# Attention beside a gated MLP on one core: the last of four pattern tiles made in place by a DMA that adds a constant

## The chip, the cores and the metric

The kernel runs on one core of a Trainium2 chip. The metric is the device time in microseconds of one execution; lower is better. A time is the median of several executions. One further execution is recorded by the hardware profiler; its lines are quoted as the profile prints them, with PE for TensorE, PEld for its weight loads, DVE for VectorE, ACT for ScalarE, POOL for GpSimd and SP for SyncE.

## The reference

One block of attention and one gated block read the same 2048 rows of 512, and a sigmoid gate mixes them:

```
q, k, v = split((x @ wqkv), 32 heads of 16)
scores  = einsum("bhqd,bhkd->bhqk", q, k) * 16 ** -0.5
a = merge_heads(softmax(scores) @ v) @ wo
b = ((x @ w_gate) * (x @ w_up)) @ w_down        # inner width 1376
g = sigmoid((x * gate_w).sum(-1, keepdims=True))
out = g * a + (1 - g) * b
```

All inputs and the output are bfloat16.

## The kernel before, in words

**Tiling.** The 2048 queries are four chunks of 512, the 32 heads are four blocks of eight, and of a block either the even or the odd four heads are taken together: that is a "quad", 32 in all. For a quad the 2048 keys are 16 key tiles of 128. One quad with one key tile is a "step", 512 in all, and a step has four score tiles of 128 keys x 512 queries, one for each head. The PE array is used as two halves of 64 rows, each split in four groups of 32 columns: `pe64` (L1616) issues a set of four matmuls on one half (recorded at L1620).

**Two ways to an exponential.** An A step goes to ScalarE: `exp` (L1709, recorded at L1718) reads one or two score banks and writes bfloat16 tiles. A D step goes to VectorE: `dpass` (L1747, recorded at L1754) adds a constant to the scaled score and writes it as int16, whose bits are read as a bfloat16; this is a piecewise linear exponential. To make it better, four such tiles with different "patterns" are used. The first is the tile y itself, 128 x 2048 int16 for the four heads. The three others are y + 32, y + 64 and y + 96, which are a quarter, a half and three quarters of an octave further. Each is multiplied with its own scaled copy of V (`Vs`), and the four products are summed on PE. `copy` (L1756) makes the others, on DVE (recorded at L1760) as a whole or on POOL (L1764) as a whole or in halves, each into a tile buffer of its own. There are eight such buffers in `DB`, and the buffers `wv` and `wk` join them once their weights are no longer needed. D steps are allowed for six of the 16 key tiles of a quad (`dks`); those that are not taken so are done on ACT.

**PV.** `pv` multiplies a finished pattern tile with V and adds it into PSUM bank 7 until a quad's 16 key tiles are done. An A step needs one PV set for each half, a D step four.

**What sets the order.** `_Sched` is a planner in Python that runs when the kernel is built. It goes through time with assumed durations, hands each engine its next piece of work, and so writes a fixed list of instructions for each engine. `_Plan.emit` (L48) turns the dependences between the lists into semaphore waits. On the chip each engine works through its list in order and waits where an operand isn't there yet. The planner's choices are steered by tables in `PAR` (L2055): each is a list of (number of windows, value), a window being 4 us of planned time. The tables named later: `acc` (L2057), how many first D steps of a quad get the treatment below; `alook` and `alook2` (L675, L700), how many score tiles for ACT may be outstanding when scores are put ahead of PV and fill work, and behind it; `dl` and `dend` (`next_d`, L218), how many D steps a quad may take and when it stops.

On POOL, `try_pool` (L972) takes a step's missing copies from the last pattern backwards; on DVE, `copy_dve` (L908) takes them from the first forwards. POOL's queue also holds the multiplications that normalise the output (recorded at L1923). SP's queue holds almost all transfers: the masked queries (`QM<-qraw`), the denominators, the rows of `oc`, weights and results.

**A path that is switched off.** With `acc` over 0, a step that is marked (L244, L245) makes only patterns two and three by `copy`. Once PV of the first pattern is done on both halves and both copies are made (`y_unref`, L506), `acc_pool` (L960) has POOL issue a DMA that adds 96 to the tile y in place:

```
src = bass.AP(c.tensor, c.offset, [[0, 128], [1, 2048]])
return self.P.dma("pool", lambda e: e.dma_start(self.db[buf], src, accum_op=ALU.add),
                  deps + [self.r["cst"]], "dacc%d" % buf)
```

The source is one row of 2048 int16 in device memory, read for every partition. In the planner POOL is taken for `aiss` 0.9 us, the tile is booked as ready `alat` 3.9 us after that, and two such tiles at least 2.65 us apart:

```
self.pool_v = self.lock_v = self.now + self.par["aiss"]
t = self.dma_v = max(self.pool_v + self.par["alat"], self.dma_v + 2.65)
for r in (0, 1):
    self.vq[r].append((t, e, 3, [op]))
```

The other work (projections, the gated block, the output projection) fills PE between scores and PV, in sets of the same shape, and DVE empties its banks.

Of the kernel before, what the change touches and what calls it, by code (L numbers as in the profile page):

```python
# [1548 lines left out]
class _Hw:  # L1549
# [376 lines left out]
    def prologue(self):  # L1926
# [119 lines left out]
        if self.par["acc"]:  # L2046
# [7 lines left out]

PAR = {'NA': 14,  # L2055
 'ND': 8,
 'acc': 0,  # L2057
 'adel': 0.1,
 'aiss': 0.9,
 'alat': 3.9,  # L2060
 'alook': ((13, 2), (5, 6), (8, 4), (6, 2), (9, 4), (3, 5), (21, 2), (3, 3), (3, 2), (1, 4), (5, 2), (18, 5),
           (6, 2), (6, 4), (5, 5), (13, 2), (4, 5), (6, 2), (2, 4), (3, 3), (7, 4), (26, 6), (7, 2)),
 'alook2': ((18, 4), (5, 3), (9, 0), (6, 2), (3, 0), (3, 3), (3, 0), (5, 5), (1, 3), (2, 0), (5, 6), (11, 3),
            (3, 5), (9, 3), (6, 2), (6, 6), (6, 5), (1, 4), (29, 0), (4, 6), (5, 2), (7, 0), (10, 4), (10, 0),
            (13, 4)),
 'amax': ((7, 5), (35, 4), (6, 5), (81, 4), (6, 5), (45, 4)),
 'amin': ((7, 3), (6, 2), (13, 4), (6, 2), (9, 3), (3, 2), (6, 4), (2, 2), (22, 3), (28, 4), (5, 3), (18, 4),
          (7, 3), (5, 4), (5, 2), (19, 4), (5, 3), (5, 4), (9, 3)),
 'apick': ((38, 0), (6, 1), (3, 0), (6, 1), (2, 0), (2, 1), (4, 0), (12, 1), (1, 0), (12, 1), (5, 0), (1, 1),
           (5, 0), (14, 1), (11, 0), (25, 1), (14, 0), (6, 1), (13, 0)),  # L2070
 'ares': ((5, 1), (6, 2), (3, 1), (21, 2), (3, 1), (6, 2), (7, 1), (1, 2), (8, 1), (17, 2), (15, 1), (6, 0),
          (24, 2), (9, 1), (9, 0), (22, 2), (18, 1)),
 'await': ((2, 0.05), (10, 0), (6, 0.05), (5, 0), (6, 0.2), (3, 0), (3, 0.2), (3, 0.1), (3, 0.2), (3, 0),
           (7, 0.05), (1, 0.2), (8, 0.05), (11, 0), (3, 0.2), (6, 0), (3, 0.4), (6, 0.05), (3, 0.1), (10, 0),
           (5, 0.4), (4, 0.2), (10, 0.05), (1, 0.4), (3, 0), (15, 0.05), (2, 0.2), (19, 0.05), (3, 0.4),
           (8, 0), (8, 0.2)),
 'cpmax': ((2, 10), (9, 6), (24, 8), (3, 5), (6, 8), (11, 2), (5, 3), (11, 6), (1, 5), (10, 10), (17, 14),
           (3, 2), (19, 8), (1, 14), (5, 6), (6, 14), (2, 10), (5, 5), (22, 8), (12, 3), (6, 8)),
 'dact': ((13, 2), (13, 3), (18, 2), (16, 3), (12, 2), (30, 3), (19, 2), (4, 3), (22, 2), (14, 3), (1, 2),
          (12, 3), (6, 2)),  # L2080
 'dahead': ((7, 0), (34, 1), (14, 0), (35, 1), (3, 0), (4, 1), (5, 0), (59, 1), (10, 0), (9, 1)),
 'dend': ((2, 2), (3, 3), (2, 1), (10, 0), (6, 3), (1, 4), (2, 1), (11, 4), (7, 3), (6, 2), (21, 3), (6, 4),
          (3, 0), (7, 4), (2, 2), (3, 4), (10, 0), (9, 4), (10, 2), (1, 3), (15, 1), (5, 3), (5, 2), (14, 0),
          (1, 4), (12, 3), (6, 2)),
 'dks': [2, 4, 7, 9, 12, 14],
 'dl': ((2, 3), (3, 4), (2, 6), (5, 4), (5, 6), (3, 5), (62, 6), (5, 4), (7, 6), (5, 5), (3, 6), (5, 4),
        (10, 6), (5, 5), (5, 6), (4, 5), (5, 6), (1, 5), (10, 6), (5, 4), (9, 6), (10, 5), (9, 6)),
 'dlook': ((29, 1), (3, 2), (70, 1), (9, 2), (1, 1), (15, 2), (13, 1), (2, 2), (19, 1), (5, 2), (14, 1)),
 'dlook2': ((2, 0), (11, 3), (5, 0), (14, 1), (6, 2), (6, 1), (8, 2), (5, 4), (4, 0), (2, 4), (8, 3), (3, 0),
            (8, 1), (5, 4), (3, 0), (2, 3), (10, 2), (9, 1), (10, 0), (4, 1), (4, 0), (11, 4), (2, 1), (5, 3),  # L2090
            (5, 0), (5, 4), (5, 0), (18, 3)),
 'dmaq': 2.0,
 'dmax': ((5, 2), (18, 3), (3, 2), (15, 3), (14, 2), (16, 3), (3, 2), (3, 3), (3, 2), (3, 3), (7, 2), (8, 3),
          (4, 2), (9, 3), (29, 2), (2, 3), (5, 2), (19, 3), (1, 2), (3, 1), (10, 2)),
 'dpair': ((17, 1), (6, 2), (3, 0), (15, 1), (14, 0), (13, 1), (6, 2), (9, 0), (4, 2), (7, 0), (1, 2), (2, 1),
           (5, 2), (9, 0), (10, 1), (10, 0), (6, 1), (10, 0), (18, 1), (1, 0), (14, 1)),
 'dpri': ((13, 1), (31, 0), (20, 1), (1, 0), (6, 1), (26, 0), (5, 1), (40, 0), (5, 1), (25, 0), (8, 1)),
 'dresv': ((67, 0), (7, 1), (7, 2), (99, 0)),
 'dwait': ((2, 0.4), (11, 0), (5, 0.2), (5, 0.4), (3, 0.1), (12, 0.2), (6, 0), (7, 0.2), (1, 0), (8, 0.2),
           (11, 0.4), (3, 0.2), (9, 0.4), (6, 0.2), (8, 0.1), (14, 0), (10, 0.2), (21, 0.4), (5, 0),  # L2100
           (14, 0.2), (6, 0.1), (3, 0), (1, 0.1), (9, 0)),
 'fcf': ((7, 1), (34, 0), (3, 1), (136, 0)),
 'fdebt': ((2, 0), (12, -10), (12, 25), (6, -30), (9, 0), (1, -30), (6, 0), (12, -10), (5, 25), (6, -30),
           (3, 0), (9, 25), (3, 10), (9, 0), (7, 25), (9, 0), (10, 10), (8, 25), (6, 0), (2, 10), (5, -10),
           (5, 10), (14, 25), (5, 0), (1, 10), (3, -10), (10, 10)),
 'ffn0': 2.6,
 'ffn1': 31.5,
 'flead': ((2, 160), (3, 0), (15, 80), (3, 160), (15, 80), (6, 160), (7, 20), (1, 160), (8, 20), (2, 80),
           (9, 10), (6, 80), (15, 160), (10, 10), (5, 40), (4, 160), (18, 80), (5, 20), (3, 0), (3, 20),
           (7, 160), (14, 80), (13, 40), (6, 80)),  # L2110
 'fmax': ((18, 3), (8, 2), (18, 3), (6, 2), (21, 1), (12, 2), (9, 3), (10, 1), (19, 3), (1, 2), (5, 3),
          (10, 2), (43, 3)),
 'fres': ((44, 0), (16, 2), (29, 0), (13, 2), (28, 0), (2, 2), (10, 1), (38, 0)),
 'fs2': ((13, 1), (22, 0), (3, 1), (6, 0), (20, 1), (10, 0), (6, 1), (3, 0), (6, 1), (3, 0), (9, 1), (20, 0),
         (4, 1), (10, 0), (5, 1), (22, 0), (18, 1)),
 'fstart': ((20, 2), (6, 1), (1, 2), (15, 1), (18, 2), (2, 1), (9, 2), (3, 1), (13, 2), (7, 1), (39, 2),
            (4, 1), (43, 2)),
 'fuse': 0,
 'fv': ((7, 1), (10, 0), (10, 1), (5, 0), (12, 1), (16, 0), (11, 1), (18, 0), (23, 1), (27, 0), (8, 1),
        (14, 0), (19, 1)),  # L2120
 'g0': 3,
 'gdue': 1.5,
 'gfull': ((2, 0.9), (24, 0.6), (6, 0.3), (9, 1.9), (3, 0.9), (3, 1.6), (4, 0.3), (16, 1.6), (10, 2.5),
           (15, 1.2), (10, 1.6), (15, 0.3), (14, 1.9), (4, 0.9), (5, 0.6), (7, 0.3), (14, 0.6), (1, 0.3),
           (5, 1.2), (13, 0.6)),
 'ghalf': ((7, 0.7), (1, 0.5), (17, 1.2), (1, 0.7), (15, 0.5), (3, 0.9), (3, 0.3), (5, 1.2), (1, 0.9),
           (14, 0.3), (5, 0.7), (6, 0.5), (5, 0.7), (19, 0.3), (19, 0.5), (8, 0.7), (5, 0.5), (6, 9),
           (7, 0.5), (10, 1.2), (8, 0.3), (2, 0.5), (13, 1.2)),
 'gwin': ((18, 0), (8, 1.2), (18, 0.5), (7, 1.2), (2, 0.5), (6, 1.2), (3, 0.2), (21, 1.2), (7, 0), (11, 1.2),
          (10, 0.5), (14, 1.2), (4, 0.5), (2, 1.2), (9, 0.8), (2, 0.5), (5, 1.2), (5, 0), (14, 0.5), (1, 1.2),  # L2130
          (13, 0)),
 'hold': 1,
 'klead': 0.9,
 'kp': [1, 4, 7],
# [3 lines left out]
 'npre': 0,  # L2138
 'olead': 0.9,
 'ov': [[], [], [], []],  # L2140
 'pfirst': ((22, 0), (4, 1), (12, 0), (33, 1), (3, 0), (28, 1), (5, 0), (12, 1), (2, 0), (9, 1), (32, 0),
            (10, 1), (8, 0)),
 'ph': 1,
 'pool0': 13.0,
 'pre0': 25.0,
# [7 lines left out]
 'retire2': 150.0,  # L2153
 'retire3': 50.0,
 'rmarg': 0.3,
 'skew': ((18, 3), (5, 2), (12, 4), (3, 2), (3, 4), (6, 2), (15, 3), (5, 2), (14, 6), (1, 2), (5, 4), (3, 3),
          (2, 1), (10, 3), (19, 1), (8, 2), (3, 6), (4, 4), (4, 6), (7, 1), (14, 3), (6, 1), (13, 2)),
 'skewd': ((2, 4), (11, 2), (14, 3), (8, 4), (3, 1), (3, 4), (3, 2), (8, 3), (29, 2), (8, 3), (12, 2), (1, 3),
           (19, 4), (4, 3), (3, 2), (12, 1), (7, 4), (5, 3), (11, 2), (4, 4), (3, 3), (10, 4)),
 'sp0': 19.5,  # L2160
 't0': 8.2,
 'tw': [(('wk', False), 0), (('wq', False), 0), (('wk', True), 20), (('wq', True), 22), (('wv',), 12),
        (('gw',), 13.5)],
 'tx': [6.5, 12, 16.5, 20.5],
 'ugdur': 1.131,
 'vpref': ((13, 2), (64, 0), (15, 3), (9, 0), (1, 2), (24, 0), (3, 1), (8, 0), (3, 1), (27, 0), (13, 3)),
 'warmto': 0.0,
 'wgap': 1.2,
 'xd': ((7, 20), (6, 6), (7, 4), (3, 2), (3, 6), (18, 2), (16, 20), (2, 2), (9, 4), (3, 6), (18, 4), (9, 6),
        (1, 20), (19, 2), (4, 4), (4, 2), (6, 4), (5, 8), (7, 2), (14, 6), (5, 2), (14, 6)),  # L2170
 'xk': ((5, 4), (7, 2), (1, 4), (4, 0), (7, 1), (2, 4), (16, 1), (2, 4), (3, 2), (5, 0), (10, 4), (11, 0),
        (1, 2), (9, 1), (14, 0), (5, 4), (5, 3), (10, 1), (14, 4), (6, 1), (3, 0), (7, 3), (14, 0), (5, 3),
        (1, 4), (5, 1), (8, 4)),
 'xq': 0,
 'xw': 0}


def bass_gated_mix__mha_block__glu_gated_bilinear__prompt_kernel(
    nc: bass.Bass,
    A_x: bass.AP,  # L2180
    A_wqkv: bass.AP,
    A_wo: bass.AP,
# [41 lines left out]
```

## Time and profile before

| | us |
|---|---|
| median of 3 executions | 710.07 |
| their range | 707.67 to 713.38 |
| the profiled execution | 708.04 |
| its span, first to last instruction | 706.3 |
| ACT busy in it | 684.8 |
| DVE busy | 645.9 |
| POOL busy | 450.7 |

The granted clock of TensorE is 1.00 throughout. Busy times count an engine's instructions as the profiler records them; PE's matmuls overlap, so that its busy time is not a measure of how full it is. In a group's line the count follows the x, then come busy time, mean nanoseconds of one, idle time of the engine just before such an instruction, and what ended that idle time. In a wait line come total, number and longest.

### The profile page before, as it was taken

How to read it: one execution, taken by the hardware profiler on the slowest of the kernel's cores; microseconds unless marked ns; L12 is line 12 of the kernel's file. 1: busy time of each engine (PE TensorE's matmuls, PEld its weight loads, DVE VectorE, ACT ScalarE, POOL GpSimd, SP SyncE). 2: the span in 40 equal slices, each digit the busy share in tenths (PEclk: the TensorE clock that was granted, in tenths of full speed). 3: DMA queues.
4: the chain of work that ended last, by engine and by line, in shares of the span. 5: the costliest groups of instructions: out<-in, count | busy, mean ns of one | idle time of the engine just before them, and what ended most of it. 6: DMA issues, size and time to landing. Idle time of an engine off the chain costs nothing.

```text
span 706.3 us, 47734 instructions
## 1 busy us (share of the span) xinstructions
PE 692.3 (98%) x22103; PEld 358.7 (51%) x22103; DVE 645.9 (91%) x1060; ACT 684.8 (97%) x820; POOL 450.7 (64%) x351
## 2 busy tenths in 40 slices
PE   8999999999999999999999999999999999999997
PEld 4564555554444545554554445555553555555553
DVE  5999999899999999999998998999999978989985
ACT  6899999999999999999999999999999999999994
POOL 3365658877464666655675747777666788487630
PEclk9999999999999999999999999999999999999999
DMA  9202341003010100001000010100001010000101
GB/s 156 69 6 57 78 107 36 6 20 94 16 35 5 35 18 23 28 11 28 13 23 23 15 33 19 36 13 13 27 7 40 12 36 24 14 23 18 29 19 33
DMA packets 33752, 22.97 MB, mean 33 GB/s; under 512 B 19500, under 2 KB 30156, under 8 KB 33552
## 3 DMA queue, kind: packets, MB, share of 16 engines
q1 hardware_dynamic: 32416, 18.86, 11.1%
q8 instruction: 173, 2.83, 1.6%
q0 software_dynamic: 176, 0.53, 0.3%
q10 hardware_dynamic: 960, 0.52, 0.3%
q14 instruction: 27, 0.22, 0.1%
HBM read 11.71 MB, written 2.36 MB: 20 GB/s over the span
## 4 chain that ended last, share of the span: by engine, by line
PE 90%; DVE 3%; ACT 3%; issue 1%; DMA 1%; ACTq 0%; DVEq 0%
PE ps L1620 90%; DVE DB L1754 2%; ACT xT L1718 1%; ACT PT L1718 1%; DVE DB L1760 1%; DMA DB<-in_A_x_dram 1%; ACT wu L1718 0%; DVE wv L1754 0%; DVE oc L1830 0%; DVE hT L1902 0%; PE ps L2017 0%; ACTq L1933 0%; DVE wu L1813 0%; ACT wd L1718 0%; ACT QM L2030 0%
## 5 line engine op out<-in xcount | busy, mean ns | idle before, releaser
L1620 PE MATMUL ps<-QM,KT 64*32 64x512 bf16 x8192 | 496.6, 379 | 4.2 <-issue 1.3
L1764 POOL TENSOR_TENSOR DB<-DB,cadd 128x512 int32<-128x512 int32 (+1 forms) x207 | 280.2, 1373 | 146.9 <-DVE DB L1760 62.0
L1718 ACT ACTIVATE PT<-ps 128x1024 bf16<-128x1024 f32 (+1 forms) x394 | 358.5, 1016 | 1.6 <-PE ps L1620 0.7
L1754 DVE TENSOR_SCALAR DB<-ps 128x512 int16<-128x512 f32 (+1 forms) x493 | 327.7, 692 | 31.8 <-PE ps L1620 28.3
L1620 PE MATMUL ps<-DB,Vs 64*17 64x512 bf16 x2856 | 261.6, 377 | 0.7
L1718 ACT ACTIVATE xT<-ps 128x1024 bf16<-128x1024 f32 (+1 forms) x270 | 258.6, 1043 | 1.9 <-PE ps L1620 1.7
L1620 PEld LDWEIGHTS ps<-QM,KT 64*32 64x32 bf16 x8192 | 152.2, 89 | 177.9 <-ACT PT L1718 46.9
L1620 PE MATMUL ps<-PT,Vp 64*17 64x512 bf16 x1444 | 204.5, 376 | 0.3 <-issue 0.2
L1620 PE MATMUL ps<-xT,Vp 64*17 64x512 bf16 x1030 | 165.3, 376 | 0.2
L1620 PE MATMUL ps<-xT,wu 64*32 64x512 bf16 x1376 | 111.9, 377 | 0.0
L1620 PE MATMUL ps<-xT,wg 64*32 64x512 bf16 x1376 | 110.5, 377 | 1.0 <-issue 0.9
L1760 DVE TENSOR_SCALAR DB<-DB 128x2048 int16<-128x2048 int16 (+1 forms) x160 | 107.3, 701 | 0.6 <-PE ps L1620 0.2
L1620 PE MATMUL ps<-wd,hT 64*32 64x512 bf16 x1408 | 100.2, 377 | 0.1
L1620 PE MATMUL ps<-DB,Vp 64*17 64x512 bf16 x1000 | 97.0, 377 | 0.6 <-DVE oc L1830 0.2
L1620 PEld LDWEIGHTS ps<-DB,Vs 64*17 64x17 bf16 x2856 | 70.6, 87 | 37.0 <-PE ps L1620 10.5
L1718 ACT ACTIVATE wd<-ps 128x1024 bf16<-128x1024 f32 (+1 forms) x69 | 65.7, 1059 | 0.6 <-PE ps L1620 0.4
L1764 POOL TENSOR_TENSOR DB<-wv,cadd 128x512 int32<-128x512 int32 (+1 forms) x38 | 49.7, 1331 | 24.2 <-DVE wv L1754 9.6
L1620 PEld LDWEIGHTS ps<-PT,Vp 64*17 64x17 bf16 x1444 | 51.2, 87 | 17.9 <-PE ps L1620 4.6
L1764 POOL TENSOR_TENSOR wv<-DB,cadd 128x512 int32<-128x512 int32 (+1 forms) x31 | 42.1, 1371 | 19.7 <-DVE DB L1760 7.8
L1754 DVE TENSOR_SCALAR wv<-ps 128x512 int16<-128x512 f32 x72 | 47.6, 683 | 2.5 <-PE ps L1620 2.1
L1764 POOL TENSOR_TENSOR wk<-DB,cadd 128x512 int32<-128x512 int32 (+1 forms) x30 | 39.4, 1324 | 15.8 <-DVE DB L1760 11.2
L1620 PEld LDWEIGHTS ps<-xT,Vp 64*17 64x17 bf16 x1030 | 40.8, 87 | 11.6 <-PE ps L1620 2.6
(108 smaller groups left out, 839.5 us busy)
## 6 DMA issues: line engine op xcount, KB each, us to landing
rb<-rscr SPq DMA_DIRECT2D x16, 256.0 KB
QM<-qraw SPq DMA_DIRECT2D x124, 16.0 KB, 2.3
oc<-oraw SPq DMA_DIRECT2D x60, 32.0 KB, 2.2
out_dram<-ost SPq DMA_DIRECT2D x12, 128.0 KB, 1.7
wd<-in_B_w_down_dram SPq DMA_DIRECT2D x10, 128.0 KB, 2.5
wu<-in_B_w_up_dram SPq DMA_DIRECT2D x12, 96.0 KB, 2.2
wg<-in_B_w_gate_dram SPq DMA_DIRECT2D x12, 96.0 KB, 2.6
wv<-in_A_wqkv_dram POOLq DMA_DIRECT2D x1, 512.0 KB, 5.2
```

Of the source, the lines that this page charges most:

```text
L1620: o = pe.matmul(dst, lhs, rhs, start=st, stop=sp, tile_position=(64 * r, 32 * cc), skip_group_check=True)
L1718: return self.P.op("act", lambda a: a.activation(dst, src, ACT.Exp, scale=self.ES), deps)
L1754: return self.dve(lambda v: v.tensor_scalar(dst, src, self.YB, 0.0, ALU.add, ALU.max), deps)
L1760: return self.dve(lambda e: e.tensor_scalar(o, a, 32.0 * v, None, ALU.add), deps)
L1764: lambda e: e.tensor_tensor(o.bitcast(I32), a.bitcast(I32), self.cadd[:, v, :].bitcast(I32).to_broadcast([128, n]), ALU.add),
```

## The change

The code of the kernel stays as it is; only the dictionary `PAR` changes. `acc` becomes a table instead of 0, so that the path described above is taken for the first two to four D steps of a quad (the entry that holds at the planned time), with 1 in two windows. In a marked step one of the three copies is not made, the DMA on POOL takes its place, and the step needs three tile buffers instead of four. In the prologue one POOL memset and two small stores on SP write the row of 96s. All other tables of the planner are replaced as well, so that the order of work on every engine is a different one, while scalars such as `aiss` and `alat`, the list `dks` and the number of buffers stay. Means over the 180 windows, before and after: `acc` 0 and 3.28, `alook` 3.59 and 2.26, `alook2` 2.49 and 3.90, `dl` 5.56 and 5.61, `dend` 2.21 and 1.97.

```diff
 PAR = {'NA': 14,
  'ND': 8,
- 'acc': 0,
+ 'acc': ((2, 2), (3, 3), (2, 2), (10, 3), (20, 4), (29, 3), (1, 4), (3, 3), (14, 4), (2, 3), (4, 4), (27, 3),
+         (25, 4), (6, 2), (19, 3), (4, 4), (5, 2), (1, 1), (1, 4), (2, 2)),
  'adel': 0.1,
  'aiss': 0.9,
  'alat': 3.9,
- 'alook': ((13, 2), (5, 6), (8, 4), (6, 2), (9, 4), (3, 5), (21, 2), (3, 3), (3, 2), (1, 4), (5, 2), (18, 5),
-           (6, 2), (6, 4), (5, 5), (13, 2), (4, 5), (6, 2), (2, 4), (3, 3), (7, 4), (26, 6), (7, 2)),
...
+ 'alook': ((122, 2), (3, 4), (42, 2), (10, 6), (3, 2)),
...
- 'dl': ((2, 3), (3, 4), (2, 6), (5, 4), (5, 6), (3, 5), (62, 6), (5, 4), (7, 6), (5, 5), (3, 6), (5, 4),
-        (10, 6), (5, 5), (5, 6), (4, 5), (5, 6), (1, 5), (10, 6), (5, 4), (9, 6), (10, 5), (9, 6)),
...
+ 'dl': ((2, 3), (3, 5), (16, 6), (1, 4), (2, 6), (3, 5), (11, 6), (3, 5), (3, 4), (2, 5), (16, 6), (4, 5),
+        (4, 6), (4, 5), (3, 6), (8, 5), (2, 4), (1, 5), (14, 6), (5, 5), (9, 6), (1, 5), (46, 6), (1, 4),
+        (2, 5), (1, 3), (4, 5), (2, 3), (2, 5), (5, 6)),
...
```

## The prediction, made before the changed kernel was run

> **What bounds the kernel now.** I read the page's busy table first, then the groups with each shape apart for ACT and POOL, then the busy times by stage, then the wait lists of PE's loads and of POOL, and last the DMA issues.
>
> ```profile
> PE 692.3 (98%) x22103; PEld 358.7 (51%) x22103; DVE 645.9 (91%) x1060; ACT 684.8 (97%) x820; POOL 450.7 (64%) x351
> 300.00:325.00 25.00, 25.00 (x872) 13.70 (x864) 24.36 (x41) 25.00 (x28) 14.02 (x15) 1.00 0.07 16
> 425.00:450.00 25.00, 25.00 (x860) 13.55 (x855) 22.34 (x34) 25.00 (x29) 19.07 (x11) 1.00 0.10 25
> ```
>
> The columns of the stage lines after the length are PE, PEld, DVE, ACT and POOL busy, granted clock, DMA share and GB/s. ACT has no idle time in most stages between 50 and 675 us; its idle is at the two ends. PE's 98% is not PE at its peak: the same page counts 22103 matmuls in sets of four, two half-arrays run side by side, and sets on one half start 0.216 us apart in the timeline (301.29, 301.50, 301.72), so 22103/4/2 x 0.216 = 597 us would hold them. PE's queue stands in between, and for whom is in its wait list:
>
> ```profile
> PEld ps L1620 <- ACT PT L1718: 47.4, 187, 0.8
> PEld ps L1620 <- ACT xT L1718: 35.3, 131, 0.8
> PEld ps L1620 <- DVE DB L1754: 31.7, 130, 0.6
> PEld ps L1620 <- PE ps L1620: 29.0, 91, 0.6
> ...
> PEld ps L1620 <- ACT wd L1718: 7.1, 30, 0.4
> PEld ps L1620 <- DVE wv L1754: 4.9, 20, 0.5
> ```
>
> It waits for score banks that ACT's exp (L1718) or DVE's passes (L1754) have not emptied. The four-pattern copies stand almost nowhere: PE waits for DVE's copies (L1760) 0.9 us in all, and in the answer on POOL's copies (L1764) the list of who waited for them is empty. POOL itself waits for others about 255 us.
>
> ```profile
> L1760 DVE TENSOR_SCALAR DB<-DB 128x2048 int16<-128x2048 int16 x150 | 103.0, 717 | 0.6 <-PE ps L1620 0.2
> ...
> L1764 POOL TENSOR_TENSOR DB<-DB,cadd 128x1024 int32<-128x1024 int32 x81 | 152.3, 1893 | 79.2 <-DVE DB L1760 32.7 <-PE ps L1620 27.3 <-DVE DB L1754 13.7
> L1764 POOL TENSOR_TENSOR DB<-DB,cadd 128x512 int32<-128x512 int32 x126 | 128.0, 1039 | 67.7 <-DVE DB L1760 29.4 <-PE ps L1620 18.6 <-DVE wv L1760 14.1
> ```
>
> So the time is ACT's score tiles plus two ends. By shape ACT has 649 exps of two tiles and 158 of one: 1456 tiles, 364 of the 512 steps (quad, key tile). DVE's passes by shape are 486 + 72 + 20 of one tile (into DB, wv and wk) and 7 of two: 592 tiles, so 148 D steps, 4.6 per quad. A step on ACT costs (684.8 - 8)/364 = 1.86 us of it. Whatever the change does, the end moves only if ACT gets fewer steps, or if PE's queue stands longer.
>
> **The change part by part.** The sum is made against the profiled execution, 708.04 us (span 706.3 and 1.74 around it); the median of the runs shown, 710.07, lies 2.0 above it. The forecast is the median plus the sum (a profiled execution would stand 2 lower).
>
> How many tiles. The acc table's mean over its 180 windows of 4 us is 3.28; times 32 quads is 105; a quad that has fewer D steps than its entry loses some, so I take 100 of the 444 copies (148 x 3; by the groups DVE made 219 whole and 15 half, POOL 118 whole and 199 half, which gives 226.5 + 217.5 = 444).
>
> Removed: POOL takes a step's copies from the last backwards, so the ones removed are mostly POOL's: 424.5 us over 217.5 tiles is 1.95 each, 195 us; if they were all DVE's it would be 157/226.5 = 0.69 each, 69 us. Directly this is worth nothing: nobody waits for POOL's copies.
>
> Added on POOL: 100 DMA issues. The nearest rows are POOL's two own DMA issues, 0.757 us (wv) and 0.913 us (gw), so 76 to 91 us. POOL is left with some 110 us more.
>
> Moved: with these 110 us POOL can make 110/1.95 = 56 copies that DVE makes now, 39 us of DVE. That could become D steps in place of A steps: one costs DVE 4 x 0.685 and half of its copies, 1.5 x 0.69, together 3.8, so ten steps, each 1.86 us off ACT: 19 us at best. PE pays six more sets each, 10 x 6 x 0.216/2 = 6.5 us, of 109 us that its queue now stands. At worst it is nothing: the tables that ration D steps hardly differ (dl 5.56 before, 5.61 after, in the mean). Between 0 and -19 I take -6, three steps, as the row it is nearest to is the rationing, which barely moves.
>
> The landing. The last pattern's PV can't be ordered against a copy of 0.6 to 1.9 us any more. It needs, in turn: PV of the first pattern on both halves and both other copies (they read the tile), POOL's turn (behind up to 1.89 us of a copy), the issue, and the landing. The order is written for 0.9 us of issue and 3.9 us after it, 4.8 in all, and 2.65 us between two of them. No row shows a DMA that adds. The nearest is POOL's plain 512 KB load, 5.2 us to landing in a stage where the DMA engines were 85% busy; POOL's 1 KB load took 4.2.
>
> ```profile
> wv<-in_A_wqkv_dram POOLq DMA_DIRECT2D x1, 512.0 KB, 5.2
> ...
> gw<-in_gate_w_dram POOLq DMA_DIRECT2D x1, 1.0 KB, 4.2
> ```
>
> From below, 4.2 is early by 0.6 and costs nothing. From above, the tile must be read as well as written; page part 3 gives 2.83 MB for 1.6% and 0.53 MB for 0.3% of 16 engines' span, 0.57% per MB, so 0.5 MB is 2.1 us of all engines and a second movement makes 7.3, late by 2.5. I take 5.2, late by 0.4, as it has the same queue and size. PE issues in order, so a late PV stops both halves, and behind it wait scores that feed ACT and DVE. If each of 100 were due at once: 40 us. Ready PVs of other steps are booked ahead of many; I let two in five show: +16.
>
> POOL's queue: behind an accumulate that waits for PV stand the next steps' copies and 16 normalisations (L1923, 1.28 us). Their cover is that nobody waits for POOL's copies now; if it goes, the price is that of a late PV and is within the 16. SP's queue is not passed; its transfers (QM 2.3 us, oc 2.2) share engines with 100 x 2.1 = 210 us of new transfers, 30% of the span on a present 13.4% by part 3; they run a quad ahead, 22 us, so 0. The y tile stays held till the landing, but a step takes three tiles, not four: 0. Prologue: one more memset and two 2 KB stores on SP, none before the first scores: 0.
>
> The order. All tables of the written order are new. First-rank lookahead of ACT's scores falls from a mean of 3.59 to 2.26, so PVs and fills go ahead of scores once two are out; second-rank rises from 2.49 to 3.90. Two tiles are one exp of 1.07 us. From ACT's idle after PE (under 10 us) to 0.03 us at each of some 800 exps, this is 0 to +24, and better pairing (158 single exps at 0.62, 0.53 each in pairs) could give -14. I take +2. Sum: -6 + 16 + 2 = +12, **722 us**.
>
> Two pages of the Trainium skill bear on it. DMA: Bandwidth & Descriptors (section "Anatomy of one DMA — SWDGE (gpsimd) path") fits such a DMA as 2.0 us plus bytes over 436 GB/s: 3.2 us for 512 KB, with an issue of 0.8 about 4.0, an estimate under the 4.8 booked. By it the landing would cost nothing and the sum would be -4; the row here, 5.2, disagrees, though among other traffic. SBUF — State Buffer (section "Who interferes with whom") says that descriptor generation on GpSimd is starved while DVE runs a two-port copy. POOL's 88.7 us of idle until DVE's copies agrees with a plan that keeps the two apart; if they still meet, each issue would lengthen by one DVE copy, and the landing with it.
>
> **The rivals.** First, faster: the landing is in time (4.8 or under from issue), and the freed DVE time does become D steps. For it: PE waits 38.9 us for passes, which fewer copies on DVE bring forward, and the DMA engines are nearly idle now (mean 33 GB/s). Against: the rationing tables. -8 to -19, so 14 off: 696 us. It decides if ACT's steps fall below about 360. Second, no difference: the relief is POOL's, which nobody waits for, and the landing is hidden behind other PVs; 703 to 717, 710. Third, much slower: the adding transfer needs 7.3 us, late by 2.5; two in five of 100 is 100 us: 810. With one in three late by half of that it is 41 us, 751, so it counts from 742 up. For it: the tile moves twice. Against: issues are some 6.5 us apart, so they don't queue. Fourth, that DVE is not relieved at all since POOL stands waiting for PVs with the copies queued behind: DVE's copies stay near 220, the forecast without the -6, 728; it lies inside the forecast's own range and shares its chance.
>
> **How the numbers follow.** Late landing, with or without relief: 0.56, 715 to 742. Faster rival: 0.25. No difference: 0.13. Much slower: 0.06. A measurement of this kernel can tell about 1%. Faster 0.25, same 0.13, slower 0.62. The range leaves out the much slower case and the better part of the faster one: 694 to 742; for the forecast alone 715 to 742.
>
> **What would show it.** Landings of the adding DMA over 4.8 us, PE's loads waiting for a DMA into DB, wv or wk in the wait list (some 16 us, more than 40 times), ACT idle some 12 us more in the middle stages, and POOL's L1764 down from 311 instructions: then the steps are right. Wrong: no PE wait for a DMA; or ACT with under 1430 tiles and the span shorter by what that saves.

## The result, and the profile after

The changed kernel takes 846.76 us in the median of four executions, against 710.29 for the kernel before on the same chip: a ratio of 1.182, with a 95% interval of 1.167 to 1.197. Two of the four, 834.2 and 845.1 us, count as undisturbed: the ratio and every difference below use their mean, 839.7 us, while the profile shows the execution of 848.43 us, with a span of 846.7. The forecast of 722 us had the sign right and the size wrong by a factor of more than ten; 742 us, the upper end of the range, is far exceeded.

The page of the changed kernel, busy times, clock and DMA queues:

```profile
PE 732.0 (86%) x22247; PEld 383.1 (45%) x22247; DVE 638.4 (75%) x1042; ACT 697.9 (82%) x976; POOL 464.7 (55%) x386
...
PEclk9999899999999999999899999999999999999988
...
q0 software_dynamic: 15872, 57.68, 37.3%
q1 hardware_dynamic: 32420, 18.87, 9.0%
q8 instruction: 174, 2.85, 1.4%
```

No engine is full any more: ACT fell from 97% to 82%. POOL's DMA queue q0 grew from 0.53 MB to 57.68, and its packets take 37% of the time of all 16 DMA engines. The line to keep in mind is q8, 174 packets of 16 KB: instructions. It stood in the page of before as well:

```profile
q8 instruction: 173, 2.83, 1.6%
q0 software_dynamic: 176, 0.53, 0.3%
```

The waits of PE's weight loads, of the matmuls and of ACT in the changed kernel (waiter, whom for, total, times, longest):

```profile
PEld ps L1620 <- issue: 105.5, 134, 3.7
PEld ps L1620 <- PE ps L1620: 38.7, 118, 1.0
PEld ps L1620 <- DVE DB L1754: 32.7, 129, 1.1
PEld ps L1620 <- ACT PT L1718: 28.4, 109, 1.4
PEld ps L1620 <- DMA DB<-cscr: 28.1, 29, 2.5
```

```profile
PE ps L1620 <- issue: 64.0, 47, 3.2
PE ps L1620 <- DMA DB<-cscr: 17.3, 19, 2.2
```

```profile
ACT PT L1718 <- PE ps L1620: 77.3, 71, 7.2
ACT xT L1718 <- PE ps L1620: 38.7, 28, 4.2
```

Before, PE stood for ACT; now ACT stands for PE. And PE stands mostly for "issue", that is, for nothing that the profile shows: 105.5 us on the loads, where it was 13.7 before:

```profile
PEld ps L1620 <- issue: 13.7, 31, 1.6
```

The new DMA into the tiles (`DMA DB<-cscr`) is there too, with 28.1 and 17.3 us, but it is the smaller part. The landings, by median and by range, in the DMA issues and in the answer on the line of the new DMA:

```profile
DB<-cscr POOLq DMA_DIRECT2D x85, 512.0 KB, 6.7
wk<-cscr POOLq DMA_DIRECT2D x14, 512.0 KB, 5.7
wv<-cscr POOLq DMA_DIRECT2D x10, 512.0 KB, 8.9
```

```profile
DMA to landing us min/median/max: 4.9/6.7/10.7
```

Even the earliest is later than the 4.8 us that the order books. The DMAs also queue among themselves: of the 108 that follow another, 36 are issued less than 2.9 us after it, which is the time that one tile holds a DMA engine (below), and these land 8.5 us after their issue, by the median, against 5.9 for the rest (computed from the trace). What "issue" is can be read from the chain of waits, here from 120 to 152 us (start, length, what):

```profile
122.67 1.81 issue
124.48 5.01 PE ps L1620 x108
129.49 0.01 issue
129.50 8.43 PE ps L1620 x265
137.93 1.99 issue
139.91 3.88 PE ps L1620 x128
143.80 2.86 issue
146.66 5.15 PE ps L1620 x159
```

From the stop of 1.81 us to the one of 1.99 PE does 108 + 265 = 373 matmuls on this chain, nearly three times 128, and then 128 up to the next. A matmul and its weight load are two instructions, and 2 x 22247 over 174 packets is 256 instructions in a packet: one packet of q8 holds 128 matmuls. I compared the start times of the weight loads with the ends of q8's packets in the trace; a stop is here more than 0.6 us between the starts of two weight loads. The changed kernel has 105 stops, and 56 of them, 101 us in all, end 0.9 to 2.0 us after the end of an instruction packet, by the median 1.4 us. In the kernel before there are 13 such stops, 11 us. Their place tells what they are: with the semaphore instructions counted in, 50 of the 56 stand at one and the same place among every 256 instructions of PE's queue, and of the 49 other stops only one does. There PE goes over to its next packet, and it stops because that packet has come late.

### The profile page after: what moved, and what is told of

Read it like the earlier page. It is cut to its first block, busy times and chain, and to the rows that moved or that the text cites. A ratio compares the mean times of both kernels' runs of the same rounds, so it can differ in the third digit from the quotient of the medians.

```text
span 846.7 us, 48048 instructions
## 1 busy us (share of the span) xinstructions
PE 732.0 (86%) x22247; PEld 383.1 (45%) x22247; DVE 638.4 (75%) x1042; ACT 697.9 (82%) x976; POOL 464.7 (55%) x386
## 3 DMA queue, kind: packets, MB, share of 16 engines
q0 software_dynamic: 15872, 57.68, 37.3%
## 4 chain that ended last, share of the span: by engine, by line
PE 51%; DMA 23%; DVE 11%; issue 9%; POOL 3%; SPq 1%; ACT 1%; ACTq 0%; DVEq 0%; POOLq 0%
PE ps L1620 51%; DMA DB<-cscr 14%; DVE DB L1754 5%; DMA rscr<-rec 3%; DMA rb<-rscr 3%; POOL DB L1764 2%; DMA QM<-qraw 2%; DVE DB L1760 2%; DVE wk L1754 1%; DVE wv L1754 1%; DMA wk<-cscr 1%; DMA wg<-in_B_w_gate_dram 1%; SPq L1825 1%; DMA DB<-in_A_x_dram 0%; DVE oc L1830 0%
## 5 line engine op out<-in xcount | busy, mean ns | idle before, releaser
L1620 PE MATMUL ps<-QM,KT 64*32 64x512 bf16 x8192 | 562.6, 391 | 43.8 <-issue 35.4
L1718 ACT ACTIVATE PT<-ps 128x1024 bf16<-128x1024 f32 (+1 forms) x519 | 398.9, 853 | 78.5 <-PE ps L1620 77.3
L1754 DVE TENSOR_SCALAR DB<-ps 128x512 int16<-128x512 f32 x489 | 324.6, 688 | 115.5 <-PE ps L1620 112.4
L1620 PE MATMUL ps<-DB,Vs 64*17 64x512 bf16 x3064 | 294.1, 391 | 30.0 <-DMA DB<-cscr 17.3
L1764 POOL TENSOR_TENSOR DB<-DB,cadd 128x512 int32<-128x512 int32 (+1 forms) x156 | 235.1, 1563 | 115.5 <-PE ps L1620 43.7
L1620 PEld LDWEIGHTS ps<-QM,KT 64*32 64x32 bf16 x8192 | 185.1, 93 | 204.1 <-issue 52.8
L1718 ACT ACTIVATE xT<-ps 128x512 bf16<-128x512 f32 (+1 forms) x285 | 215.1, 830 | 39.5 <-PE ps L1620 38.7
L1771 POOL DMA_DIRECT2D DB<-cscr x85 | 77.8, 957 | 105.4 <-PE ps L1620 71.6
L1620 PEld LDWEIGHTS ps<-DB,Vs 64*17 64x17 bf16 x3064 | 79.3, 88 | 86.4 <-DMA DB<-cscr 28.1
L1764 POOL TENSOR_TENSOR wv<-DB,cadd 128x512 int32<-128x512 int32 (+1 forms) x24 | 35.6, 1499 | 36.5 <-PE ps L1620 23.9
L1754 DVE TENSOR_SCALAR wk<-ps 128x512 int16<-128x512 f32 x64 | 42.4, 685 | 10.6 <-PE ps L1620 9.9
L1620 PEld LDWEIGHTS ps<-xT,wg 64*32 64x32 bf16 x1376 | 37.1, 94 | 24.5 <-DMA wg<-in_B_w_gate_dram 6.2
```

What stands on the lines that cost most here:

```text
L1620: o = pe.matmul(dst, lhs, rhs, start=st, stop=sp, tile_position=(64 * r, 32 * cc), skip_group_check=True)
L1718: return self.P.op("act", lambda a: a.activation(dst, src, ACT.Exp, scale=self.ES), deps)
L1754: return self.dve(lambda v: v.tensor_scalar(dst, src, self.YB, 0.0, ALU.add, ALU.max), deps)
L1764: lambda e: e.tensor_tensor(o.bitcast(I32), a.bitcast(I32), self.cadd[:, v, :].bitcast(I32).to_broadcast([128, n]), ALU.add),
```

## The experiments

Three theories were put against each other. A: the late landings themselves cost the time, as the last pattern's PV waits in PE's queue. B: the traffic costs it, as PE's instruction fetches (and SP's transfers) stand behind the adding packets on the same DMA engines. C: the new order of work is slow by itself. All ratios are to the kernel before, measured beside each, 709.5 to 710.2 us.

**The landing not waited for.** The tile is added to as before, but PV of the last pattern reads keys in its place, and the landing only delays the reuse of the tile.

```diff
-            self.vq[r].append((t, e, 3, [op]))
+            self.vq[r].append((t, e, 3, []))
...
+        if e.acc and v == 3:
+            return [("k",)] * 4          # KT[lo:hi, 0, 0:512]
```

> The changed kernel in which PV of the last pattern reads a fixed block of keys in place of the tile, so that it does not wait for the DMA; the DMA is still issued, moves as much, and its landing only frees the buffer (the output leaves out the last pattern of 109 steps). Theory A, the late landings themselves (4.9 to 10.7 us against 4.8 booked) cost the time: 715 to 740 us, no issue stops on PE beyond the 14 us of before. Theory B, the traffic costs it, as PE's instruction fetches and SP's transfers stand behind the adding packets: 780 to 830 us, PE's stops put down to issue stay near 100 us. Theory C, the new order is bad by itself: above 800 us.

Measured: 830.7 us, 1.171 (1.158 to 1.185). Theory A has no place for this: no PV waits for the adding DMA any more, and 121 us (830.7 against 709.5) remain of 129 (839.7 against 710.3). In this kernel's waits PE's loads stand just as long for "issue":

```profile
PEld ps L1623 <- issue: 117.8, 144, 3.8
```

**The DMA replaced by an addition on POOL, on half of the tile.**

```diff
-        return self.P.dma("pool", lambda e: e.dma_start(self.db[buf], src, accum_op=ALU.add), ...)
+        a = self.db[buf][:, 0:1024].bitcast(I32)
+        return self.P.op("pool", lambda e: e.tensor_tensor(a, a, <96 in both halves>, ALU.add), ...)
```

> The changed kernel with the DMA replaced by POOL adding the constant in place to half of the tile, 1.04 us, about what the issue takes (the output leaves out the other half of the last pattern). No adding DMA, same order, same dependences. Theories A and B: 700 to 720 us, as both need the DMA. Theory C, the order: above 780 us.

Measured: 704.6 us, 0.992 (0.985 to 0.999). The same order with the same dependences and no adding DMA is no slower than before, so theory C is out, and what the DMA costs against this kernel is 839.7 - 704.6 = 135 us. PE's loads wait for ACT again (53.7 us), and ACT is at 97%:

```profile
PE 689.3 (98%) x22247; PEld 362.6 (52%) x22247; DVE 635.3 (90%) x1042; ACT 682.8 (97%) x976; POOL 477.8 (68%) x386
```

**acc at 0, with all other new tables.** Only `'acc': 0` in the new `PAR`; the planner writes another order.

> The changed kernel with acc at 0 and all other new tables kept: the order is written anew by the planner without the adding DMA. Theories A and B: 715 to 750 us (tables made for another use of POOL fit less well). Theory C: above 780 us.

Measured: 744.0 us, 1.049 (1.041 to 1.057). The new tables fit the adding DMA and are 5% worse without it, yet still 96 us better than with it on the chip.

**A plain write in place of the addition.** `accum_op` is taken out, and the tile is overwritten with the constant.

> The changed kernel with the same DMA writing its constant row over the tile and not adding it (the last pattern's tile is then wrong). Landing shows what the adding costs: if the tile's second movement is what makes it late, the landing falls from 6.7 to about 5 us, and the time to 740 to 780 us by theory A and to 760 to 800 by theory B; if a plain write lands as late, the time stays at 830 to 850.

Measured: 772.6 us, 1.089 (1.086 to 1.093), within what B gave and also within what A gave. What tells them apart is the landing:

```profile
DB<-cscr POOLq DMA_DIRECT2D x85, 512.0 KB, 4.6
```

It is about in time, 4.6 us against 4.8 booked (over all 109 tiles 4.7 in the median, 3.6 to 6.8), PE's loads wait for it 1.8 us in all, and still 68 us are lost against the kernel with the addition on POOL. In the trace's DMA records an adding packet of 4 KB takes 0.328 us in the median, a plain one 0.159 (0.358 and 0.193 in the mean). Both transfers move 57.68 MB by the page; the adding one holds the engines about twice as long.

**Half of the bytes.** The DMA adds to columns 0 to 1023 only.

> The changed kernel with the adding DMA over half of the tile, 256 KB (the other half of the last pattern is left out). Theory B in its sharper form, that PE stands because its instruction fetches, 16 KB every 128 matmuls, wait on their DMA engine behind the adding packets of 0.328 us, eight in a row per tile: four in a row are 1.3 us, most of which the fetch's head start hides, so 715 to 750 us and PE's stops put down to issue under a third of the 64 us of the changed kernel. If only the number of transfers mattered and not their length: 800 us and more.

Measured: 764.8 us, 1.077 (1.072 to 1.081). That is above the 750 us that theory B gave: the loss more than halves but does not vanish, and less of it is hidden than I had expected.

**Two DMAs of half the columns each.**

```diff
+        for h in (0, 1):
+            dst = self.db[buf][:, 1024 * h : 1024 * h + 1024]
+            d = self.P.dma("pool", lambda e, dst=dst: e.dma_start(dst, src, accum_op=ALU.add), ...)
```

> The changed kernel with the same bytes added by two DMAs of half the columns each, issued one behind the other (the output is whole). If the fetch can get in between two DMAs of one queue, it waits for 1.3 us in place of 2.6: 750 to 800 us in spite of one more issue of 0.87 us on POOL for each tile. If it waits till both are through: 840 to 880 us.

Measured: 884.0 us, 1.245 (1.241 to 1.248): worse, and just above the upper range. PE's stops for "issue" are somewhat fewer, but its loads and matmuls now wait 67.1 and 50.0 us for DMAs into `DB`, and the issues take 1.2 us each in the median, twice per tile. Nothing shows that a fetch gets in between the two: one in ten begins 3.82 us or more after PE has gone over to the packet before, and in the changed kernel that is 3.85.

**Rows cut into four descriptors of 1 KB.** The source is read as `[[0, 128], [0, 4], [1, 512]]`.

> The changed kernel with one adding DMA whose rows are cut into four pieces of 1 KB (the output is whole). If a fetch waits behind the bytes on its engine: 830 to 860 us, as in the changed kernel. If it can get in between shorter pieces: under 800 us. If the issue on POOL grows with the number of pieces: its 0.87 us rises, and the time with it.

Measured: 1220.1 us, 1.718 (1.712 to 1.723), far beyond all that was expected. A 1 KB piece takes 0.167 us in the mean, so a tile holds each engine for 32 x 0.167 = 5.3 us in place of 8 x 0.358 = 2.9, the landing is 14.6 us, and the issue on POOL grew from 0.87 to 1.30 us. PE now stands mostly for the tiles, 242.9 us on its loads, so that this run is no measure of the fetches.

**Junk traffic to device memory.** No tile is touched by a DMA: PV of the last pattern reads the first tile as it is, and POOL issues a plain copy of `rows` blocks of 16 x 4 KB to memory that nobody reads. With 8, 4 and 2 blocks the trace shows mostly 8, 4 and 2 such packets in flight at once, which fits one DMA engine for each block.

```diff
+        dst = bass.AP(self.junk.tensor, ..., [[16 * 2048, rows], [2048, 16], [1, 2048]])
+        src = bass.AP(c.tensor, c.offset, [[0, rows], [0, 16], [1, 2048]])
+        return self.P.dma("pool", lambda e: e.dma_start(dst, src), ...)
```

> The changed kernel without the addition: PV of the last pattern reads the first tile as it is (the output leaves out the constant of 109 steps) and waits for no DMA; in place of the adding DMA POOL issues a plain copy of 1 MB into device memory that nobody reads, as 16 blocks of 16 rows of 4 KB. Its blocks are meant to go to 16 DMA engines, 16 rows each, some 2.6 us per engine and issue, as the adding DMA has. Theory B (PE stands since its instruction fetches wait behind the packets on the same engine): PE's issue stops as in the changed kernel, time 780 to 840 us. If the stops came from traffic to the tiles in SBUF: 705 to 720 us.

> The same with 8 blocks of 16 rows, 512 KB, meant to go to 8 of the 16 DMA engines with the same 16 rows on each. If a fetch waits only for packets on its own engine, the result is one of two: about as many issue stops as with 16 blocks if PE's fetches use one of these 8 engines, almost none (705 to 725 us) if they use another; if fetches are spread, about half of the loss. If what counts is the bytes moved in all, half of the loss as well. Should the blocks go to 16 engines with 8 rows each: like the half-sized transfer, 750 to 770 us.

> The junk copy with 4 blocks of 16 rows, 256 KB, on 4 DMA engines (with 8 blocks, at most 8 packets were in flight at once for most of the time, and PE's issue stops stayed near those of 16 engines' traffic). If PE's fetches use one fixed engine: either as many issue stops as with 8 blocks, 73 us on PE and 800 us or more, or nearly none, 705 to 720 us. If the fetches are spread evenly over 16 engines: a quarter of the full loss, some 730 to 745 us.

> The same with 2 blocks of 16 rows, 128 KB, on 2 engines. One fixed engine: the full stops, 800 us or more, or nearly none, 705 to 715 us. Spread evenly: 715 to 725 us with some 15 us of issue stops.

Measured: 1062.3 us with 16 blocks, 815.5 with 8, 759.8 with 4, 736.9 with 2. Sixteen came out far above what B had given, with each 4 KB packet at 0.282 us in the mean in place of the 0.19 of the plain write and of the smaller junk copies. From 8 to 2 blocks the loss against 704.6 about halves with each step: 111, 55, 32 us. So the tiles are not needed for the loss at all. One engine for PE's fetches with the blocks always on the same engines is excluded, since that would give all or nothing. An even spread fits in kind, but 759.8 and 736.9 us lie above the 745 and 725 that I had given for it. The traces do not name the engines, so it stays open whether the fetches move over them or the blocks do. Here are the matmuls' stops with 16 blocks, and then with 2:

```profile
PE ps L1622 <- issue: 227.9, 60, 6.7
```

```profile
PE ps L1622 <- issue: 19.7, 25, 2.3
```

All runs in one table. "Engine time" is the mean packet time times the packets of one issue on one engine. "After a fetch" is the sum of those PE stops over 0.6 us that end 0.9 to 2.0 us after an instruction packet, less 9.5 us that the kernel with the addition on POOL has too; both are computed from the traces of the profiled executions.

| kernel | engine time per issue, us | engines | loss against 704.6, us | after a fetch, us |
|---|---|---|---|---|
| changed | 2.9 | 16 | 135 | 92 |
| landing not waited for | 2.8 | 16 | 126 | 104 |
| plain write | 1.5 | 16 | 68 | 65 |
| half of the bytes | 1.6 | 16 | 60 | 52 |
| junk, 16 blocks | 4.5 | 16 | 358 | 257 |
| junk, 8 blocks | 3.1 | 8 | 111 | 100 |
| junk, 4 blocks | 3.0 | 4 | 55 | 46 |
| junk, 2 blocks | 3.2 | 2 | 32 | 31 |

The last two columns run together: four fifths or more of the loss stand after a fetch, except in the changed kernel, 68%, and with 16 blocks, 72%. Bytes are not the measure: the plain write and the 8 blocks both move 57.7 MB and lose 68 and 111 us, while the plain write and half of the adding bytes, 57.7 and 29 MB, hold the engines about equally long and lose about the same.

The traces also show how a packet comes late. In the kernel with the addition on POOL it begins 1.04 us after PE has gone over to the packet before it and takes 1.03 us (medians). PE starts on it never less than 1.24 us after its end, by the median 1.68, so some 0.4 us are to spare. With the adding DMA the packet itself takes no longer, 0.97 us, but it begins later: 59 of 173 begin more than 2 us after PE's step to the packet before, where 3 did, and 56 of these 59 had rows of the adding DMA in flight 1 us after that step. Of the fetches that had junk in flight at that moment, 74 of 83 began so late with 16 blocks, 46 of 71 with 8, 20 of 73 with 4 and 7 of 71 with 2, which is near the share of the 16 engines that the junk takes. That fits a fetch that waits for what its own DMA engine has in hand.

**The whole tile added on POOL.** As above, on all 2048 columns.

> The changed kernel with the adding DMA replaced by POOL adding the constant in place to the whole tile, 1.9 us where the order books 0.9 (the output is whole). From the run with half of the tile, 704.6 us, and 109 x 0.85 us more on POOL, which stood idle for over 200 us: 705 to 720 us. Theory C would make it slower than that.

Measured: 758.4 us, 1.068 (1.065 to 1.071), a miss. The addition takes 1.9 us where the order books 0.9 us of POOL, so DVE's copies, which the order keeps away from POOL's work, now run into it: 71 copies of whole tiles overlap an operation on POOL and take 1.53 us in the median, 99 do not and take 0.68, none over 0.70. With half of the tile 31 overlap. The answers on the copies' line, first this kernel, then the one with half of the tile (times are min/median/max in ns):

```profile
L1760 DVE TENSOR_SCALAR wk<-DB x11: 679/1231/2377, 207.7 to 737.3; 128x2048 int16<-128x2048 int16 x9, 128x1024 int16<-128x1024 int16 x2
```

```profile
L1760 DVE TENSOR_SCALAR wk<-DB x11: 419/683/884, 193.0 to 683.1; 128x2048 int16<-128x2048 int16 x9, 128x1024 int16<-128x1024 int16 x2
```

A copy of 0.68 us takes up to 2.4. DVE's busy time is 697 us in this kernel against 635; how much of the 54 us of time that makes was not separated. I had costed POOL's extra time at its idle time and left out whom it shuts out. No version with whole output that was run beats the kernel before.

## Why the prediction was wrong, point by point

*The bound of before* was read rightly: with the DMA gone, ACT is at 97% again and the time is within 1% of before.

*Number of tiles*: 100 taken, 109 issues in the trace.

*Removed and moved, -6*: the order without the DMA measures 704.6 against 709.5, -5; the run leaves out half of each addition, so this stands near the gain and is not the gain itself, and it holds the effect of the new order too. DVE's passes cover 616 tiles, 154 D steps, against 148: six steps moved and not three. This step held in size.

*The issue on POOL*: 76 to 91 us taken, 77.8 + 13.6 + 10.3 = 101.7 measured, 0.93 each. Right enough, and off the path.

*The landing, +16*: I took 5.2 us, as the plain row was, and kept 7.3 as the upper end because the tile moves twice. Measured is 6.7 in the median, near the upper end, and the reason given for it is borne out (0.328 us a packet against 0.159, landing 6.7 against 4.6). What waiting for it costs is the changed kernel less the one that does not wait: 839.7 - 830.7 = 9 us, and as the intervals of the two ratios overlap, it may be nothing. So the +16 is not confirmed, though the tiles are later than I took them to be: PE's waits for them overlap with its waits for instructions. The fit in the Trainium skill's DMA: Bandwidth & Descriptors (section "Anatomy of one DMA — SWDGE (gpsimd) path"), gave about 4.0 us with the issue as an estimate; the plain write here lands in 4.6, the adding one in 6.7, and the measurement decides.

*The step that failed*: "its transfers (QM 2.3 us, oc 2.2) share engines with 100 x 2.1 = 210 us of new transfers, 30% of the span on a present 13.4% by part 3; they run a quad ahead, 22 us, so 0." I asked only which of SP's transfers would be late, took an average share of the DMA engines, and set the price at nothing. The runs put 126 us of the 135 there (830.7 - 704.6, with no PV waiting for the DMA). The term also counted one movement for each tile, where the landing's upper end had counted two: q0 takes 37.3% of 846.7 us, 316 us, and not 210. The queue that mattered was on the page that I quoted from: q8, the instructions, which I used for a price per megabyte and did not read as a queue with a consumer. It has no quad of lead: PE uses up a packet every 4.1 us (706 us over 173 packets) with some 0.4 to spare, and an adding tile holds every engine for 2.9. SP's transfers were late as well (POOL stood 59 us for `rb<-rscr`, where 4.4 before), and a part of the loss outside the last column of the table may be theirs; that part was not separated and stays open.

The Trainium skill's DMA: Bandwidth & Descriptors, section "Queues, rings and completion order", says that a DMA engine takes the queues in turn but drains a whole packet of a queue, some 9 to 17 descriptors, before it turns to the next. A packet in this sense is several of those that the profile counts; the eight rows and their completion that a tile puts on each engine would be one, but no run here shows it. One fetch in ten begins at least 3.85 us after PE's step in the changed kernel and 1.55 with the addition on POOL; these 2.3 us are within the 2.9 of one tile, which agrees. With 16 blocks of junk it is 7.25, 5.7 more, over the 4.5 of one issue, so there a fetch can wait for more than one issue, or for a slower one.

*The order, +2*: theory C is out, as said; with the step above it the new order comes to -5, and the two were not told apart.

*The rivals*: the third, "much slower", had 0.06 of the chance and named the doubled movement rightly, but put its price on the late PVs; with the wait taken away most of its time stayed. What was held against it, "issues are some 6.5 us apart, so they don't queue", goes by the mean: 36 of 108 issues follow within 2.9 us of another, and their tiles land 8.5 us after issue. It also said nothing of the other queues.

*The signs that were named*: landings over 4.8 us and PE's waits for DMAs into the tiles came (28.1 us on the loads, 29 times, where some 16 us and over 40 times were named); ACT's idle grew by far more than 12 us. POOL's L1764 came down to 242 instructions; before there were 317, not the 311 that the prediction gives. These signs came with a mechanism that was not in the sum, so they did not show that the steps were right.

## What to carry to other kernels

When a change adds traffic, go through every queue on the page that shares the DMA engines and ask what lead its consumer has, the instruction queue first: a kernel of many short matmuls lives on a fresh 16 KB packet every few microseconds. Price the traffic by how long one issue holds an engine, not by its mean share or its bytes. A wait that no releaser is named for, and that comes back after a regular count of instructions, is best taken for a fetch until shown otherwise.

## What the runs showed of the hardware that was not expected

PE stops when its instruction packets are late, and traffic on the DMA engines makes them late even where it touches neither PE's tiles nor its semaphores: 815 us with 57.7 MB of junk in 8 blocks against 704.6 without. An adding packet of 4 KB holds an engine for 0.328 us and a plain one for 0.159. Rows in pieces of 1 KB take 4 x 0.167 = 0.67 us in place of 0.358 in the mean. The granted clock of TensorE was lower in the kernels with the longest times: 1.00 before, 0.96 in the changed kernel, 0.87 with 16 blocks of junk, 0.82 with the short descriptors; the mean of a score matmul went from 379 to 391 ns between the first two. The sum of the stops alone does not set it: the kernel with the whole tile added on POOL has 89 us of stops over 0.6 us at a clock of 1.00, the one with the plain write 90 us at 0.99. What the clock adds to the time was not measured.
